# A longer pitch for the x, r and g tiles of an attention and feed-forward kernel, and two buffers of combined weight words

## The chip, the core and the metric

The kernel runs on one core of a Trainium2 chip. A core has five engines that run beside each other and wait for one another by semaphores: TensorE (PE; its weight loads are listed apart as PEld), VectorE (DVE), ScalarE (ACT), GpSimd (POOL) and SyncE (SP), whose queue starts nearly all transfers here. The on-chip memory has 128 partitions; an address in this document is a byte offset within each partition. The metric is device time in microseconds; less is better.

## What is computed

Linear attention over 8 batches, 8 heads, 576 positions and head size 64, and then a feed-forward network on its output (4608 tokens, 512 wide, 2048 hidden):

```python
q_s = exp(q - max(q, -1));  q_s = q_s / (sum(q_s, -1) + 1e-9)
k_s = exp(k - max(k, 2));   k_s = k_s / (sum(k_s, 2) + 1e-9)
kv = einsum('bhsd,bhse->bhde', k_s, v)
attn = einsum('bhsd,bhde->bhse', q_s, kv)
x = attn.transpose(0, 2, 1, 3).reshape(4608, 512)
h = x @ w_in
r = maximum(h, 0)
g = r * r
out = g @ w_out
```

All is float32, in and out.

## The kernel before

**Precision.** TensorE multiplies in the fast form of float32 (`F32R`). To keep accuracy, every operand of the feed-forward part is split in two: `hi`, the value cast to F32R, and `lo`, what is left. A product is made of three matmuls: hi × hi, hi × lo and lo × hi.

**Tiling.** Tokens go in 9 blocks: block 0 to 7 hold 512 of each batch's 576 positions, and block 8 the 64 left over of each batch, which attention parks in DRAM (`x_left`). x of a block lies in `x_hi` and `x_lo`, tiles of 128 partitions × 4 chunks (`cc`) × 512 tokens. There are two of each, and block `blk` uses number `blk % 2`: `x_hi0`, `x_lo0` in even blocks, `x_hi1`, `x_lo1` in odd ones. The second pair is made late (L527, L528), in the space that the tiles of the start (`first`) leave. A chunk of x is 512 × 4 = 2048 bytes, and each chunk follows the last at once.

The hidden width goes in 16 chunks (`fc`). One step is one block and one chunk, so there are 9 × 16 = 144 steps. A step is

- `ffn_h` (L412 to L414): for each of 4 chunks `cc`, three matmuls with 128 × 128 weights from `wi[fc]` as the loaded operand and x as the moving one, 512 columns: hi × x_hi, hi × x_lo, lo × x_hi. Twelve in all, called the x part below.
- `activate`: ScalarE takes the bank to `r` (L418, relu); VectorE squares it in place (L424; L422 in block 0); ScalarE casts it to `g_hi` (L425); VectorE, in most steps of block 0 GpSimd, subtracts to get `g_lo` (L429).
- `ffn_out` (L446 to L448), two steps later (`LAG`): for each of 4 groups of tokens, three matmuls with 128 columns of `g_hi`, `g_hi`, `g_lo` as the loaded operand and the 512 columns of `wo[fc]` hi, lo, hi as the moving one. Twelve in all, called the output part.

So a step has 24 matmuls of 512 columns, and each has a weight load of its own. All wi and wo stay on the chip: 4096 bytes each, 2048 of hi and 2048 of lo.

**Weights at the start.** During the start and block 0 each of the 32 weight chunks is made from raw bits by `split_weight`: ScalarE and VectorE combine the words in a buffer `w` (VectorE, L173, writes it last), then ScalarE casts it to the hi part (L180) and GpSimd subtracts to get the lo part (L181). `w` rotates over `WB` = 3 buffers of 2048 bytes.

**Attention** of the next block is cut into units that a table of numbers (`STEADY_AT`, `EARLY_AT`) puts between the steps. Its last matmuls (L384) have 320 or 256 columns, with `kvs` loaded and `qs` moving, and its results are split into the next block's x tiles. Block 7 only makes block 8's x from the parked tokens (`left_units`, L192 and L195), and block 8 has no attention beside it.

The order on each engine comes from a scheduler at build time. Tiles are laid out in the order of their pools, one after the other.

Of the kernel before, what the change touches and what calls it, by code (L numbers as in the profile page):

```python
# [8 lines left out]
F32 = mybir.dt.float32  # L9
F32R = mybir.dt.float32r  # L10
# [6 lines left out]
P = 128  # L17
# [2 lines left out]
HIGH = 4  # L20
BLK = 32
PAD = 8

half = slice(0, HALF), slice(HALF, P)
FLT_MAX = float.fromhex("0x1.fffffep127")
RAWB, WB = 4, 3

BESIDE = 4
EARLY_SPLITS = [("o",0),("o",1)]
# [16 lines left out]
def attention_ffn_kernel(ctx: ExitStack, tc: tile.TileContext, q, k, v, w_in, w_out, out):  # L46
# [5 lines left out]
    NCC = DM // P  # L52
    NFC = DF // P
    NT = 512
# [3 lines left out]
    const = ctx.enter_context(tc.tile_pool(name="const", bufs=1))  # L58
    work = ctx.enter_context(tc.tile_pool(name="work", bufs=2))
# [5 lines left out]

    stay = ctx.enter_context(tc.tile_pool(name="stay", bufs=1))
    raws, wi, wo = {}, {}, {}
    x_hi = [const.tile([P, NCC, NT], F32R, name="x_hi0")]
    x_lo = [const.tile([P, NCC, NT], F32R, name="x_lo0")]
    x_left = dram.tile([P, NCC, B * LEFT], F32, name="x_left")  # L70


# [25 lines left out]
    ones = const.tile([P, 1], F32, name="ones")  # L98
    const.tile([P, PAD], F32, name="pad_back")

# [313 lines left out]
        last.append(nc.tensor.matmul(ps, wi[fc][:, 1, sl], xh[:, cc, :], start=False, stop=(cc == NCC - 1)))  # L414

    def activate(ps, blk, fc):
        r = work.tile([P, NT], F32, name="r")
        nc.scalar.activation(r, ps, AF.Relu)  # L418
        g_hi = work.tile([P, NT], F32R, name="g_hi")
        g_lo = work.tile([P, NT], F32R, name="g_lo")  # L420
        if blk == 0:
            nc.vector.tensor_tensor(r, r, ps, op=ALU.mult)  # L422
        else:
            nc.vector.tensor_tensor(r, r, r, op=ALU.mult)  # L424
        gh = nc.scalar.copy(g_hi, r)  # L425
        if blk == 0:
            his.append(gh)
        e = nc.gpsimd if blk == 0 and fc < G_LOW_POOL else nc.vector
        e.tensor_tensor(g_lo, r, g_hi.bitcast(F32), op=ALU.subtract)  # L429
        return g_hi, g_lo  # L430

    def ffn_h(blk, fc):
        ps = next_bank("h" if blk else "first")
        for cc in range(NCC):
            h_part(ps, blk, fc, cc)
        return activate(ps, blk, fc)
# [87 lines left out]
    start_done.append(1)  # L524
    ps_o = ctx.enter_context(tc.tile_pool(name="ps_o", bufs=4, space=bass.MemoryType.PSUM))
    late = ctx.enter_context(tc.tile_pool(name="late", bufs=1))
    x_hi.append(late.tile([P, NCC, NT], F32R, name="x_hi1"))  # L527
    x_lo.append(late.tile([P, NCC, NT], F32R, name="x_lo1"))  # L528

    for pr in range(NB):  # L530
        load_pair(1, pr)
# [34 lines left out]
    for n in range(len(steps) + LAG):  # L566
        if n < len(steps):
            blk, fc = steps[n]
            if n < PRE:
                gs[n] = activate(hs[fc], blk, fc)  # L570
            else:
                gs[n] = ordered(ffn_h, blk, fc) if blk == 0 else ffn_h(blk, fc)
            if blk == 0:
                for x in [n + 4] if n else range(5):
                    if PRE <= x < NFC and order0[x] not in wi:
                        split_weight("i", order0[x])
                for x in [n + 2] if n else range(3):
                    if x < NFC and order0[x] not in wo:
                        split_weight("o", order0[x])
                finish_split()  # L580
        m = n - LAG
        in_slot(2 * n)
        if m >= 0:
            b2, f2 = steps[m]
            if m % NFC == 0:
                accs[b2] = [ps_o.tile([P, DM], F32, name=f"o_ps{t}", tag="o") for t in range(4)]
            args = b2, f2, gs.pop(m), accs[b2], m % NFC
            ordered(ffn_out, *args) if b2 == 0 else ffn_out(*args)
        in_slot(2 * n + 1)
# [30 lines left out]
```

## Time and profile before

| | us |
|---|---|
| median of 2 runs | 899.95 (899.69 to 900.2) |
| profiled execution | 900.7 |
| span of the profiled execution, first to last instruction | 898.9 |
| TensorE busy in it | 869.5 |
| mean granted TensorE clock | 0.994 |

The profile is of one execution. Its views used here are: the page (busy time by engine, 40 slices of the span, the chain of work that ended last), the windows (busy time by engine in a stretch), the groups by line and shape (busy us and mean ns of one, then the idle time of the engine ahead of them and what ended it), and the timeline (start in us, duration in us, engine, line, operation, tiles). A line number is that of the kernel before. A matmul's duration in the timeline overlaps the next one's, as TensorE is a pipeline and the ends are modelled; how fast matmuls go is read from the distance of their starts.

### The profile page before, as it was taken

The page shows a single profiled execution, that of the slowest core. Times are in us where ns is not written, and L with a number is a line of the kernel's source. Part 1 is how long each engine was busy: PE and PEld are TensorE (multiplying, and loading weights), DVE is VectorE, ACT ScalarE, POOL GpSimd, SP SyncE. Part 2 cuts the span into 40 slices and gives each one's busy share as a digit, 9 for nine tenths or more (in the row PEclk, how much of TensorE's full clock was granted, in tenths as well). Part 3 has the DMA queues.
Part 4 walks back from the last instruction along what each step waited for, and adds up shares of the span by engine and source line. Part 5 has one row for each costly group of instructions (what it writes and reads, how often), then busy time and mean ns, then how long its engine had stood idle before and what let it go on. Part 6 is the DMA issues. An engine that isn't in the chain of part 4 may idle for free.

```text
span 898.9 us, 12680 instructions
## 1 busy us (share of the span) xinstructions
PE 869.5 (97%) x4368; PEld 700.6 (78%) x4368; DVE 579.6 (64%) x1177; ACT 407.7 (45%) x801; POOL 202.4 (23%) x177
## 2 busy tenths in 40 slices
PE   4997999999999999999999999999999999999997
PEld 3675677888888888888888888888888888888885
DVE  7767898877778876877688767876764242222222
ACT  3785756455345453544454544454444232222222
POOL 3676634222212220231122212221222000000000
PEclk9998999999999999999999999999999999999999
DMA  9999212422142224322333133222311030002001
GB/s 234 278 317 257 68 30 58 117 77 79 44 117 76 80 58 104 85 71 71 88 84 81 51 83 88 77 66 69 92 31 32 2 93 1 1 1 47 1 1 47
DMA packets 95743, 73.18 MB, mean 81 GB/s; under 512 B 47552, under 2 KB 85440, under 8 KB 95680
## 3 DMA queue, kind: packets, MB, share of 16 engines
q1 hardware_dynamic: 94944, 71.53, 29.5%
q10 hardware_dynamic: 736, 0.85, 0.4%
q8 instruction: 34, 0.56, 0.3%
q14 instruction: 29, 0.24, 0.1%
HBM read 54.00 MB, written 18.35 MB: 80 GB/s over the span
## 4 chain that ended last, share of the span: by engine, by line
PE 85%; DVE 1%; issue 0%; ACT 0%
PE o_ps L446 14%; PE bank L412 14%; PE o_ps L448 14%; PE o_ps L447 14%; PE bank L414 13%; PE bank L413 13%; PE bank L305 2%; PE bank L384 1%; DVE w L173 0%; DVE r L422 0%; DVE bank L172 0%; DVE m L243 0%; DVE kvn L321 0%; DVE o_last L460 0%; DVE m L246 0%
## 5 line engine op out<-in xcount | busy, mean ns | idle before, releaser
L412 PE MATMUL bank<-x_hi,wi 128*128 128x512 f32 x568 | 226.0, 398 | 2.2 <-DVE r L422 2.2
L446 PE MATMUL o_ps<-wo,g_hi 128*128 128x512 f32 x576 | 227.6, 397 | 0.0
L447 PE MATMUL o_ps<-wo,g_hi 128*128 128x512 f32 x576 | 224.9, 390 | 0.0
L448 PE MATMUL o_ps<-wo,g_lo 128*128 128x512 f32 x576 | 224.4, 391 | 0.0
L414 PE MATMUL bank<-x_hi,wi 128*128 128x512 f32 x568 | 223.4, 393 | 0.0
L413 PE MATMUL bank<-x_lo,wi 128*128 128x512 f32 x568 | 222.4, 392 | 0.0
L424 DVE TENSOR_TENSOR r<-r 128x512 f32<-128x512 f32 x128 | 110.7, 865 | 119.5 <-ACT r L418 119.2
L429 DVE TENSOR_TENSOR g_lo<-r,g_hi 128x512 fp32r<-128x512 f32 x132 | 100.7, 763 | 106.7 <-ACT g_hi L425 105.3
L425 ACT CAST g_hi<-r 128x512 fp32r<-128x512 f32 x144 | 89.2, 619 | 124.4 <-PE o_ps L447 78.2
L418 ACT ACTIVATE r<-bank 128x512 f32<-128x512 f32 x142 | 84.7, 596 | 102.5 <-PE bank L414 99.6
L412 PEld LDWEIGHTS bank<-x_hi,wi 128*128 128x128 f32 x568 | 107.1, 189 | 26.3 <-DVE r L422 3.5
L446 PEld LDWEIGHTS o_ps<-wo,g_hi 128*128 128x128 f32 x576 | 108.2, 188 | 23.5 <-issue 0.5
L448 PEld LDWEIGHTS o_ps<-wo,g_lo 128*128 128x128 f32 x576 | 108.1, 188 | 23.2
L447 PEld LDWEIGHTS o_ps<-wo,g_hi 128*128 128x128 f32 x576 | 108.2, 188 | 22.8 <-issue 0.5
L414 PEld LDWEIGHTS bank<-x_hi,wi 128*128 128x128 f32 x568 | 106.9, 188 | 24.2 <-POOL wi L181 0.4
L413 PEld LDWEIGHTS bank<-x_lo,wi 128*128 128x128 f32 x568 | 107.0, 188 | 21.9 <-issue 0.2
L395 POOL TENSOR_TENSOR x_lo<-xf,x_hi 128x256 fp32r<-128x256 f32 x48 | 39.6, 825 | 374.0 <-ACT x_hi L394 373.3
L338 POOL TENSOR_TENSOR qs<-qT,qs 64x640 fp32r<-64x640 f32 x48 | 81.8, 1705 | 60.0 <-ACT qs L337 47.1
L224 DVE TENSOR_REDUCE m<-kt 128x128 f32<-128x640 f32 x32 | 41.4, 1298 | 20.6 <-DMA kt<-in_k_dram 20.4
L337 ACT CAST qs<-qT 64x640 fp32r<-64x640 f32 x48 | 34.9, 726 | 39.6 <-DMA qT<-bounce 39.0
L271 ACT ACTIVATE qn<-qn 128x640 f32<-128x640 f32 x32 | 23.6, 739 | 54.2 <-DVE qn L268 44.8
L386 ACT COPY xf<-bank 64x320 f32<-64x320 f32 (+1 forms) x96 | 37.9, 395 | 20.6 <-PE bank L384 13.0
(118 smaller groups left out, 775.3 us busy)
## 6 DMA issues: line engine op xcount, KB each, us to landing
out_dram<-o SPq DMA_DIRECT2D x70, 128.0 KB, 2.4
raw_i<-in_moe_w_in_dram SPq DMA_DIRECT2D x16, 512.0 KB, 8.4
raw_o<-in_moe_w_out_dram SPq DMA_DIRECT2D x16, 512.0 KB, 9.6
bounce<-tb SPq DMA_DIRECT2D x24, 320.0 KB, 2.2
qT<-bounce SPq DMA_DIRECT2D x96, 80.0 KB, 2.2
kt<-in_k_dram SPq DMA_DIRECT2D x32, 160.0 KB, 3.0
qt<-in_q_dram SPq DMA_DIRECT2D x30, 160.0 KB, 3.0
vt<-in_v_dram SPq DMA_DIRECT2D x56, 80.0 KB, 2.5
```

Source lines behind the costliest of these rows:

```text
L224: nc.vector.tensor_reduce(m, kk.rearrange("p h j d -> p h d j"), axis=AX.X, op=ALU.max)
L338: nc.gpsimd.tensor_tensor(qs[other], qT[own], qs[own].bitcast(F32), op=ALU.subtract)
L412: nc.tensor.matmul(ps, wi[fc][:, 0, sl], xh[:, cc, :], start=(cc == 0), stop=False)
L413: nc.tensor.matmul(ps, wi[fc][:, 0, sl], xl[:, cc, :], start=False, stop=False)
L414: last.append(nc.tensor.matmul(ps, wi[fc][:, 1, sl], xh[:, cc, :], start=False, stop=(cc == NCC - 1)))
L418: nc.scalar.activation(r, ps, AF.Relu)
L424: nc.vector.tensor_tensor(r, r, r, op=ALU.mult)
L425: gh = nc.scalar.copy(g_hi, r)
L429: e.tensor_tensor(g_lo, r, g_hi.bitcast(F32), op=ALU.subtract)
L446: nc.tensor.matmul(acc[t], g_hi[:, ts], wo[fc][:, 0], start=(n == 0), stop=False)
L447: nc.tensor.matmul(acc[t], g_hi[:, ts], wo[fc][:, 1], start=False, stop=False)
L448: prev = nc.tensor.matmul(acc[t], g_lo[:, ts], wo[fc][:, 0], start=False, stop=(n == NFC - 1))
```

## The change

Each chunk of the x tiles, and each of the tiles r, g_hi and g_lo, gets 64 bytes more behind its 2048 (`GAP` = 16 elements); the kernel takes the first 512 columns of it as before. A tile of 32 bytes (`pad_late`) is put ahead of `x_hi1`. The combined words `w` have two buffers and not three, which gives 2048 bytes back.

```diff
+GAP = 16
-RAWB, WB = 4, 3
+RAWB, WB = 4, 2
-    x_hi = [const.tile([P, NCC, NT], F32R, name="x_hi0")]
-    x_lo = [const.tile([P, NCC, NT], F32R, name="x_lo0")]
+    x_hi = [const.tile([P, NCC, NT + GAP], F32R, name="x_hi0")[:, :, :NT]]
+    x_lo = [const.tile([P, NCC, NT + GAP], F32R, name="x_lo0")[:, :, :NT]]
...
-        r = work.tile([P, NT], F32, name="r")
+        r = work.tile([P, NT + GAP], F32, name="r")[:, :NT]
...
-        g_hi = work.tile([P, NT], F32R, name="g_hi")
-        g_lo = work.tile([P, NT], F32R, name="g_lo")
+        g_hi = work.tile([P, NT + GAP], F32R, name="g_hi")[:, :NT]
+        g_lo = work.tile([P, NT + GAP], F32R, name="g_lo")[:, :NT]
...
-    x_hi.append(late.tile([P, NCC, NT], F32R, name="x_hi1"))
-    x_lo.append(late.tile([P, NCC, NT], F32R, name="x_lo1"))
+    late.tile([P, PAD], F32, name="pad_late")
+    x_hi.append(late.tile([P, NCC, NT + GAP], F32R, name="x_hi1")[:, :, :NT])
+    x_lo.append(late.tile([P, NCC, NT + GAP], F32R, name="x_lo1")[:, :, :NT])
```

Where the tiles begin in the built programs (bytes in each partition, and the same modulo 2048; r, g and w have several buffers):

| tile | before | modulo 2048 | after | modulo 2048 |
|---|---|---|---|---|
| x_hi0 | 1152 | 1152 | 1152 | 1152 |
| x_lo0 | 9344 | 1152 | 9600 | 1408 |
| r | 38208, 40256 | 1344, 1344 | 38720, 40832 | 1856, 1920 |
| g_hi | 42304, 44352 | 1344, 1344 | 42944, 45056 | 1984, 0 |
| g_lo | 46400, 48448 | 1344, 1344 | 47168, 49280 | 64, 128 |
| w | 63808, 65856, 67904 | 320 | 64704, 66752 | 1216 |
| wi, wo (first of 32, 4096 apart) | 80192 | 320 | 79040 | 1216 |
| x_hi1 | 211264 | 320 | 210144 | 1248 |
| x_lo1 | 219456 | 320 | 218592 | 1504 |

Chunk cc of an x tile lies 2048·cc behind its start before, and 2112·cc after: modulo 2048, all four at one place before, each 64 bytes further after.

On every engine the instructions stand in the same order in both programs; what differs is addresses, and what some wait for. The waits that are other ones are in block 0: two subtractions to g_lo on GpSimd name an earlier instruction of GpSimd itself, and the rest are in the combining of weights. Here is VectorE's queue before, around the writing of w for the first wo (SCALAR_TENSOR_TENSOR w<-raw_o is the last step of combining the words; in brackets stand the semaphores that a row waits for):

```order
L314 RECIPROCAL rs<-rs 128x1 [waits DVE_49]
L172 SCALAR_TENSOR_TENSOR bank_89<-bank_89,raw_o_165 128x512 [waits DMAHW4_49,Activation_49]
L173 SCALAR_TENSOR_TENSOR w<-raw_o_165,bank_89 128x512 [waits DVE_49]
L224 TENSOR_REDUCE m<-kt_78 128x128 [waits DMAHW5_49,DMAHW4_49]
L172 SCALAR_TENSOR_TENSOR bank_89<-bank_89,raw_o_169 128x512 [waits DMAHW6_49,Activation_49]
```

The same place after, where the lines stand one further down:

```order
L315 RECIPROCAL rs<-rs 128x1 [waits DVE_49]
L173 SCALAR_TENSOR_TENSOR bank_89<-bank_89,raw_o_165 128x512 [waits DMAHW4_49,Activation_49]
L174 SCALAR_TENSOR_TENSOR w<-raw_o_165,bank_89 128x512 [waits DVE_49,Pool_49]
L225 TENSOR_REDUCE m<-kt_78 128x128 [waits DMAHW5_49,DMAHW4_49]
L173 SCALAR_TENSOR_TENSOR bank_89<-bank_89,raw_o_169 128x512 [waits DMAHW6_49,Activation_49]
```

Nothing moved; the writing of w waits for GpSimd (Pool) too. The same is added at three more rows of this kind; at the other 28 the row waits for GpSimd already, or for nothing of it in either program, and where it waits, it is for the buffer two splits back and not three.

## The prediction

> **What bounds the kernel now.** I read the page first: busy shares, slices, the chain that ended last.
>
> ```profile
> PE 869.5 (97%) x4368; PEld 700.6 (78%) x4368; DVE 579.6 (64%) x1177; ACT 407.7 (45%) x801; POOL 202.4 (23%) x177
> ...
> PE   4997999999999999999999999999999999999997
> ...
> PEclk9998999999999999999999999999999999999999
> ...
> PE 85%; DVE 1%; issue 0%; ACT 0%
> ```
>
> TensorE is the bound from about the seventh slice on, at full granted clock, and 85% of the chain is its own work. A nanosecond more on every 512-column matmul therefore arrives at the end in full. The windows by stage say the same, and show where it is not so:
>
> ```profile
> 100.00:150.00 50.00, 47.12 (x233) 35.65 (x232) 44.64 (x91) 34.15 (x65) 26.38 (x19) 1.00 0.19 52
> 150.00:200.00 50.00, 50.00 (x256) 40.64 (x255) 39.36 (x83) 23.86 (x48) 12.07 (x9) 1.00 0.34 88
> ```
>
> (Columns: PE, PEld, DVE, ACT, POOL busy, clock, DMA share, GB/s.) Until 150 us TensorE still idles; behind it, it has no gap. So only blocks 1 to 8 (128 steps, 3072 matmuls of 512 columns) count for a price per matmul.
>
> Since no instruction moves, I then looked for anything that already depends on addresses. Block number mod 2 picks x_hi0/x_lo0 or x_hi1/x_lo1, and nothing else in the feed-forward part changes with it. The timeline of ScalarE has one L425 row per step (144 in all); these are the first of blocks 2 to 6 and 7:
>
> ```profile
> 247.35 0.62 ACT L425 CAST g_hi<-r 128x512 fp32r<-128x512 f32 x1 [1.89 <-PE o_ps L447]
> ...
> 341.62 0.62 ACT L425 CAST g_hi<-r 128x512 fp32r<-128x512 f32 x1 [1.84 <-PE o_ps L447]
> ...
> 435.30 0.62 ACT L425 CAST g_hi<-r 128x512 fp32r<-128x512 f32 x1 [1.89 <-PE o_ps L447]
> ...
> 529.56 0.62 ACT L425 CAST g_hi<-r 128x512 fp32r<-128x512 f32 x1 [1.84 <-PE o_ps L447]
> ...
> 623.11 0.62 ACT L425 CAST g_hi<-r 128x512 fp32r<-128x512 f32 x1 [1.89 <-PE o_ps L447]
> ...
> 717.39 0.62 ACT L425 CAST g_hi<-r 128x512 fp32r<-128x512 f32 x1 [1.84 <-PE o_ps L447]
> ```
>
> The differences are 94.27, 93.68, 94.26, 93.55, 94.28 us: even blocks take 0.655 us more (94.27 against 93.615), 41 ns a step. Without attention beside it the gap is cleaner. Block 7 from its 7th to its 13th step, and block 8 from its first to its last:
>
> ```profile
> 750.03 0.62 ACT L425 CAST g_hi<-r 128x512 fp32r<-128x512 f32 x1 [1.84 <-PE o_ps L447]
> ...
> 782.67 0.62 ACT L425 CAST g_hi<-r 128x512 fp32r<-128x512 f32 x1 [1.84 <-PE o_ps L447]
> ...
> 804.52 0.62 ACT L425 CAST g_hi<-r 128x512 fp32r<-128x512 f32 x1 [1.89 <-PE o_ps L447]
> ...
> 887.51 0.62 ACT L425 CAST g_hi<-r 128x512 fp32r<-128x512 f32 x1 [1.89 <-PE o_ps L447]
> ```
>
> Six steps in 32.64 us are 5.440 us each, 226.7 ns a matmul; 15 steps in 82.99 are 5.533, 230.5 ns. The same shapes at the same clock differ by 93 ns a step, and of the operands only x lies elsewhere. I call 226.7 the settled rate. How it is lost is seen one matmul at a time (timeline of TensorE, first column the start), in block 3 around an attention matmul:
>
> ```profile
> 348.98 0.39 PE L413 MATMUL bank<-x_lo,wi 128*128 128x512 f32 x1
> 349.20 0.39 PE L414 MATMUL bank<-x_hi,wi 128*128 128x512 f32 x1
> 349.43 0.31 PE L384 MATMUL bank<-qs,kvs 128*128 128x320 f32 x1
> 349.57 0.40 PE L412 MATMUL bank<-x_hi,wi 128*128 128x512 f32 x1
> ...
> 350.51 0.39 PE L413 MATMUL bank<-x_lo,wi 128*128 128x512 f32 x1
> 350.73 0.39 PE L414 MATMUL bank<-x_hi,wi 128*128 128x512 f32 x1
> 350.96 0.31 PE L384 MATMUL bank<-qs,kvs 128*128 128x320 f32 x1
> ```
>
> One foreign operand pair, and the six matmuls from 349.57 to 350.96 take 231.7 ns each. And where block 8 passes from the output part to x:
>
> ```profile
> 843.27 0.40 PE L412 MATMUL bank<-x_hi,wi 128*128 128x512 f32 x1
> 843.50 0.40 PE L413 MATMUL bank<-x_lo,wi 128*128 128x512 f32 x1
> 843.74 0.39 PE L414 MATMUL bank<-x_hi,wi 128*128 128x512 f32 x1
> ```
>
> Two intervals of together 0.47 us, 235 ns each: the dearest seen in a run of full matmuls.
>
> My reading: while a matmul streams its moving operand, the next one's weights are loaded, and how these two addresses stand to each other sets the rate. Modulo 512 bytes that distance is 0 in the output part (g loaded at 1344, wo streamed at 320) and in x parts on x_hi1 (320 and 320); in x parts on x_hi0 (1152) it is 192. With distance 0 throughout it settles; each change of distance unsettles it for some matmuls, and at 192 it does not settle.
>
> **The change part by part.**
>
> *Pitch and places of x.* As built, wi and wo start at 1216 modulo 2048. Chunk cc of x_hi0 then streams at 1152+64cc, x_lo0 at 1408+64cc, x_hi1 at 1248+64cc, x_lo1 at 1504+64cc. The distance, constant within a part before, now changes with every chunk, between hi and lo, and in odd blocks is 32 modulo 64, which no row of before shows. *Places of g.* g_hi lies at 1984 or 0, g_lo at 64 or 128: the distance to wo is now 256 or 320 for hi, 384 or 448 for lo, never 0. So no part keeps the only relation that I see settled. The price goes by two ends. Lower: odd blocks become as even ones are. Blocks 1, 3, 5: 3 × 0.655 = 1.97 us; block 7: 3 steps beside attention at 0.041 and 13 without at 0.093, 1.33 us. Sum 3.3 us. Upper: every matmul at the unsettled 231.7. Even blocks run at 230.5 (block 8's rate, taken for all), odd ones beside attention at 230.5 − 41/24 = 228.8. Blocks 2, 4, 6, 8: 1.2 × 384 × 4 = 1.84 us; blocks 1, 3, 5: 2.9 × 384 × 3 = 3.34; block 7: 72 × 2.9 + 312 × 5.0 = 1.77 us. Sum 6.9 us. I stay near the lower end, +4.1 us, since that is measured over whole blocks and the upper over six matmuls.
>
> A gain isn't excluded, as the 32-byte and 256-byte distances may settle too; that is a rival below.
>
> *Vector and scalar engines.* r, g, x and w move for them too. Here are their rows by shape in block 7:
>
> ```profile
> L424 DVE TENSOR_TENSOR r<-r 128x512 f32<-128x512 f32 x14 | 9.7, 691 | 28.4 <-ACT r L418 28.4
> L429 DVE TENSOR_TENSOR g_lo<-r,g_hi 128x512 fp32r<-128x512 f32 x14 | 9.7, 691 | 21.8 <-ACT g_hi L425 21.7
> ...
> L195 DVE TENSOR_TENSOR x_lo<-xs,x_hi 128x512 fp32r<-128x512 f32 x4 | 2.7, 690 | 2.0 <-ACT x_hi L192 2.0
> ```
>
> 691, 691 and 690 ns, though the inputs lie in three arrangements: one address twice, two tiles of equal phase, and xs against x at four different phases. I cost it at nothing; and VectorE's 28.4 us of idle time before L424 would cover a few per cent.
>
> *Two buffers of w.* L173 now waits until GpSimd's subtraction (L181) of two splits ago has read its buffer, not three. Behind the wait stands VectorE's queue in block 0, and behind that the r and k operations that TensorE waits for before 150 us. The least room that I find among 30 such pairs is this one:
>
> ```profile
> 60.32 1.30 POOL L181 TENSOR_TENSOR wi<-w,wi 128x512 fp32r<-128x512 f32 x1 [1.11 <-ACT wi L180]
> ...
> 63.34 0.69 DVE L173 SCALAR_TENSOR_TENSOR w<-raw_i,bank 128x512 uint32<-128x512 uint32 x1
> ```
>
> The read ends at 61.62, the write starts at 63.34: 1.72 us to spare. Cost 0; if that cover were gone, a 1.3 us subtraction late 30 times would be the bound, 39 us in block 0, from which these rows are far.
>
> Sum: the profiled execution took 900.7 us (span 898.9 and 1.8 around it); + 4.1 is 904.8. It stood 0.75 over the median of 899.95, so against the median 904.0.
>
> **The rivals.**
>
> *It settles better (faster).* If the new distances settle as 0 does, even blocks lose their extra: 3 × 0.655 + 16 × 0.093 = 3.5 us, 896.5. If attention matmuls no longer unsettle them either, another (228.8 − 226.7) × 384 × 6 = 4.8 us: 891.7. For it: only two distances have been seen, and one of two settles. Against: settling took a constant distance, and there is none now.
>
> *Addresses don't matter (no change).* Then 900.0. For it: the DVE rows above. Against: 5.440 and 5.533 us. [...] The trace does not agree where only x's place differs, 226.7 against 230.5 ns, so I give it less than it would have alone.
>
> *It never settles and each matmul is as dear as a first one (slower).* At 235 ns: even blocks 4.5 × 384 × 4 = 6.9 us, blocks 1, 3, 5 6.2 × 384 × 3 = 7.1, block 7 72 × 6.2 + 312 × 8.3 = 3.0; 17 us, 917. It decides against the change by over 2% only from a mean of about 235.4 ns on, with a further cost of the 32-byte shift in odd blocks.
>
> *The floor itself falls (much faster).* If 226.7 ns holds a conflict too, and the shortest interval above, 350.51 to 350.73 (0.22 us), were kept, 3072 × about 9.5 ns (from a mean of some 229.5 over blocks 1 to 8) would go: 871. Against: that short one follows a long one, and no mean of several lies below 226.7. [...]
>
> **How the numbers follow.** Unsettled more often, 901.5 to 909: 0.45. Settled better, 889 to 898.5: 0.27. No effect, within 1.5 us: 0.18. The floor falls: 0.05. Slower by over 2%: 0.05. The range 890 to 910 leaves out both last ones and the edges; the forecast's own is 901.5 to 909. About 2% is what a measurement of this kernel can tell from no change, so: faster 0.05, within 0.90, slower 0.05.
>
> **What would show it.** Right: L425 steps in block 7's end at about 5.53 us or more, where they were 5.440; blocks 3 and 5 as long as 2, 4, 6; intervals in groups of 226 to 235 ns in the output part too. L173 without a wait for GpSimd; DVE rows at 691. Wrong: steps of 5.44 in block 8 (settled better), both unchanged (no effect), any step under 5.4 (the floor), DVE or ACT rows that change, or a longer time to the first step of block 1.

## The result, and the profile after

| | before | after |
|---|---|---|
| median, us | 899.95 (2 runs) | 910.08 (2 runs, 909.85 to 910.3) |
| profiled execution, us (span) | 900.7 (898.9) | 909.85 (908.1) |
| ratio to before | | 1.0102, 95% interval 1.0082 to 1.0122 |

The changed kernel is slower by 1.0%. The forecast was 904.0, with a range of 890 to 910 and a range of its own of 901.5 to 909: the sign was right, and the size was more than double what was forecast, just outside both ranges.

The page of the kernel after has the same shape as before. TensorE's busy time has grown by 10.8 us, from 869.5; that of the other engines moved by no more than 1.2:

```profile
PE 880.3 (97%) x4368; PEld 702.7 (77%) x4368; DVE 580.8 (64%) x1177; ACT 407.8 (45%) x801; POOL 201.4 (22%) x177
...
PEclk9998999999999999999999999999999999999999
```

The clock row is that of before, and the mean granted clock is 0.995 where it was 0.994, so it is not the clock. ScalarE's timeline, the casts to g_hi (now L426, one line down) with which blocks 2 to 7 begin, one of the middle of block 7, and the first and last of block 8:

```profile
248.67 0.62 ACT L426 CAST g_hi<-r 128x512 fp32r<-128x512 f32 x1 [1.89 <-PE o_ps L448]
...
343.66 0.62 ACT L426 CAST g_hi<-r 128x512 fp32r<-128x512 f32 x1 [1.88 <-PE o_ps L448]
...
438.63 0.62 ACT L426 CAST g_hi<-r 128x512 fp32r<-128x512 f32 x1 [1.89 <-PE o_ps L448]
...
533.62 0.62 ACT L426 CAST g_hi<-r 128x512 fp32r<-128x512 f32 x1 [1.88 <-PE o_ps L448]
...
628.59 0.62 ACT L426 CAST g_hi<-r 128x512 fp32r<-128x512 f32 x1 [1.89 <-PE o_ps L448]
...
723.63 0.62 ACT L426 CAST g_hi<-r 128x512 fp32r<-128x512 f32 x1 [1.88 <-PE o_ps L448]
...
762.60 0.62 ACT L426 CAST g_hi<-r 128x512 fp32r<-128x512 f32 x1 [1.89 <-PE o_ps L448]
...
796.00 0.62 ACT L426 CAST g_hi<-r 128x512 fp32r<-128x512 f32 x1 [1.89 <-PE o_ps L448]
...
812.69 0.62 ACT L426 CAST g_hi<-r 128x512 fp32r<-128x512 f32 x1 [1.89 <-PE o_ps L448]
...
896.44 0.62 ACT L426 CAST g_hi<-r 128x512 fp32r<-128x512 f32 x1 [1.90 <-PE o_ps L448]
```

Blocks 2 to 6 take 94.99, 94.97, 94.99, 94.97 and 95.04 us: the difference between even and odd is gone, and all are longer than the longest of before (94.28). In block 7, six steps take 796.00 − 762.60 = 33.40 us, 5.567 each, where they were 5.440; in block 8, 15 steps take 83.75, 5.583 each, where they were 5.533. Against before, blocks 2, 4 and 6 have lost 0.72, 0.73 and 0.76 us, blocks 3 and 5 1.29 and 1.42, block 7 (812.69 − 723.63 = 89.06 against 87.13) 1.93, block 8 0.76 in 15 steps. With 1.44 in block 1 (from 154.18 to 248.67; before, from 154.30 to 247.35) that is 9.05 of the 9.2 us between the spans. Block 0 ends where it ended.

TensorE's timeline in block 7 after, first column the start, at the end of an x part and in the output part behind it:

```profile
764.48 0.39 PE L415 MATMUL bank<-x_hi,wi 128*128 128x512 f32 x1
764.71 0.40 PE L413 MATMUL bank<-x_hi,wi 128*128 128x512 f32 x1
...
765.41 0.40 PE L447 MATMUL o_ps<-wo,g_hi 128*128 128x512 f32 x1
765.64 0.40 PE L448 MATMUL o_ps<-wo,g_hi 128*128 128x512 f32 x1
...
766.80 0.39 PE L447 MATMUL o_ps<-wo,g_hi 128*128 128x512 f32 x1
```

Ten intervals from 764.48 to 766.80 are 232 ns each on average, across both parts. Nothing settles any more.

### The profile page after: what moved, and what is told of

Same layout as the page of the kernel before. It is cut to its first block, busy times and chain, and to the rows that moved or that the text cites. A ratio compares the mean times of both kernels' runs of the same rounds, so it can differ in the third digit from the quotient of the medians.

```text
span 908.1 us, 12684 instructions
## 1 busy us (share of the span) xinstructions
PE 880.3 (97%) x4368; PEld 702.7 (77%) x4368; DVE 580.8 (64%) x1177; ACT 407.8 (45%) x801; POOL 201.4 (22%) x177
## 4 chain that ended last, share of the span: by engine, by line
PE 87%; DMA 4%; DVE 4%; issue 1%; SPq 1%; ACT 1%; POOL 0%; DVEq 0%; POOLq 0%; ACTq 0%
PE bank L413 14%; PE o_ps L447 14%; PE bank L414 14%; PE o_ps L449 14%; PE bank L415 14%; PE o_ps L448 14%; PE bank L306 2%; DMA kt<-in_k_dram 2%; PE bank L385 1%; DMA qt<-in_q_dram 1%; DMA raw_i<-in_moe_w_in_dram 1%; DVE m L225 1%; SPq L154 1%; DVE bank L173 1%; PE first_ps L306 0%
## 5 line engine op out<-in xcount | busy, mean ns | idle before, releaser
L413 PE MATMUL bank<-x_hi,wi 128*128 128x512 f32 x568 | 227.5, 401 | 2.0 <-DVE r L423 1.9
L449 PE MATMUL o_ps<-wo,g_lo 128*128 128x512 f32 x576 | 226.9, 396 | 0.0
L414 PE MATMUL bank<-x_lo,wi 128*128 128x512 f32 x568 | 225.6, 397 | 0.0
L425 DVE TENSOR_TENSOR r<-r 128x512 f32<-128x512 f32 x128 | 112.7, 880 | 125.1 <-ACT r L419 124.7
L426 ACT CAST g_hi<-r 128x512 fp32r<-128x512 f32 x144 | 89.1, 619 | 123.2 <-PE o_ps L448 79.5
L387 ACT COPY xf<-bank 64x320 f32<-64x320 f32 (+1 forms) x96 | 38.0, 395 | 23.4 <-PE bank L385 17.4
```

Source lines behind the costliest of these rows:

```text
L413: nc.tensor.matmul(ps, wi[fc][:, 0, sl], xh[:, cc, :], start=(cc == 0), stop=False)
L414: nc.tensor.matmul(ps, wi[fc][:, 0, sl], xl[:, cc, :], start=False, stop=False)
L449: prev = nc.tensor.matmul(acc[t], g_lo[:, ts], wo[fc][:, 0], start=False, stop=(n == NFC - 1))
```

## The experiments

All have two buffers of w where nothing else is said, and all keep the order of instructions on every engine. "Distance" is the address of the weights being loaded minus that of the operand then streaming. Ratios are to runs of the kernel before on the same chip, where its median was 900.5 to 901.4 us. A step's time is read, as above, from ScalarE's casts to g_hi. The first four runs take the change apart.

**Two buffers alone.**

```diff
-RAWB, WB = 4, 3
+RAWB, WB = 4, 2
```

> The kernel before with two buffers of combined words and nothing else; all tiles behind them move by 2048 bytes, so every address modulo 2048 stays. Theory (the distance between the moving operand and the weights loaded beside it, modulo 512, sets the rate): no change, 900.0 within 0.5 us, steps of 5.440 us in block 7 and 5.533 in block 8. Rival (the loss comes from the missing third buffer): some 910, with VectorE waiting for GpSimd in block 0 and a later first step of block 1 than 154.3 us.

Measured: 901.07 us, ratio 1.0005 (0.9995 to 1.0014), steps of 5.44 and 5.53. The buffers cost nothing that can be told. In the changed kernel too VectorE does not wait for them: the profile names no wait ahead of any of its 32 rows that write w (L174). Here are GpSimd's timeline and VectorE's there, at the tightest pair of the prediction:

```profile
60.57 1.30 POOL L182 TENSOR_TENSOR wi<-w,wi 128x512 fp32r<-128x512 f32 x1 [1.10 <-ACT wi L181]
```

```profile
63.64 0.69 DVE L174 SCALAR_TENSOR_TENSOR w<-raw_i,bank 128x512 uint32<-128x512 uint32 x1
```

The read ends at 61.87, 1.77 us ahead of the write.

**All distances at 0, pitch as before.**

```diff
-    const.tile([P, PAD], F32, name="pad_back")
+    const.tile([P, PAD + 80], F32, name="pad_back")
```

> Two buffers of combined words, and 320 bytes more in the pad behind the constants, so that r, g, w, wi, wo and the odd x tiles all move by 320 and every distance, that of x_hi0 to wi too, is 0 modulo 512; pitch 2048 as before. Theory: block 8 settles, 5.44 us a step as in block 7; even blocks as long as odd ones (93.6 us); sum 896.5 within 1 us. Rival (x_hi0 is slow for its own address or for what is near it, not for the distance): 900, block 8 at 5.53.

Measured: 896.38 us, ratio 0.9959 (0.9944 to 0.9974). Here are ScalarE's first and last cast of block 8:

```profile
801.59 0.62 ACT L425 CAST g_hi<-r 128x512 fp32r<-128x512 f32 x1 [1.83 <-PE o_ps L447]
...
883.19 0.62 ACT L425 CAST g_hi<-r 128x512 fp32r<-128x512 f32 x1 [1.83 <-PE o_ps L447]
```

15 steps in 81.60 us: 5.440 each, where x_hi0 at its old distance had 5.533. x_hi0 itself did not move; the weights loaded beside it did. Nor is it the weights' own address, since odd blocks run at 5.440 with the weights at either place. So it is the distance. This kernel beats both.

**The pitch of x alone.**

```diff
-    x_hi = [const.tile([P, NCC, NT], F32R, name="x_hi0")]
+    x_hi = [const.tile([P, NCC, NT + GAP], F32R, name="x_hi0")[:, :, :NT]]
...
-    x_hi.append(late.tile([P, NCC, NT], F32R, name="x_hi1"))
+    x_hi.append(late.tile([P, NCC, NT + GAP], F32R, name="x_hi1")[:, :, :NT])
```

(x_lo likewise.)

> Two buffers of combined words, and the pitch of 2112 bytes for the x tiles alone, without the 32 bytes ahead of x_hi1; r and g as before, and their distance to wo still 0 modulo 512. Theory: the x part is unsettled in all blocks and the output part begins unsettled each time, as in block 8 of the kernel before or worse: steps of 5.53 to 5.58 us in blocks 7 and 8, 903 to 908 us. Rival (the places of g make the loss): 900 or less, block 7 at 5.44.

Measured: 905.73 us, ratio 1.0057 (1.0040 to 1.0074), 5.53 us a step in blocks 7 and 8. One x part in block 7 shows more, since its four chunks stand at four distances (TensorE's timeline):

```profile
760.80 0.39 PE L413 MATMUL bank<-x_hi,wi 128*128 128x512 f32 x1
761.03 0.39 PE L414 MATMUL bank<-x_lo,wi 128*128 128x512 f32 x1
761.25 0.39 PE L415 MATMUL bank<-x_hi,wi 128*128 128x512 f32 x1
761.48 0.40 PE L413 MATMUL bank<-x_hi,wi 128*128 128x512 f32 x1
...
762.89 0.40 PE L413 MATMUL bank<-x_hi,wi 128*128 128x512 f32 x1
```

The first chunk (hi at distance 0, lo at 256 modulo 512) keeps 0.68 us for three matmuls, 227 ns each; the six behind it (at 192 and then at 128 modulo 256) take 1.41, 235 ns each. So 256 is as good as 0, which suggested a period of 256 bytes and not 512. From here on, distances are given modulo 256.

**The pitch of r and g alone.**

```diff
-        r = work.tile([P, NT], F32, name="r")
+        r = work.tile([P, NT + GAP], F32, name="r")[:, :NT]
...
-        g_hi = work.tile([P, NT], F32R, name="g_hi")
-        g_lo = work.tile([P, NT], F32R, name="g_lo")
+        g_hi = work.tile([P, NT + GAP], F32R, name="g_hi")[:, :NT]
+        g_lo = work.tile([P, NT + GAP], F32R, name="g_lo")[:, :NT]
```

> Two buffers of combined words, and the pitch of 2112 bytes for r and g alone; x as before, so x_hi1 stands at distance 0 to wi, x_hi0 at 64 modulo 512, and g at 256 to 448 to wo. Theory: the output part is unsettled in all blocks, the x part of odd blocks can settle again: 5.47 to 5.55 us a step in block 7, 902 to 907 us. Rival (the pitch of x or the 32 bytes make the whole loss): 900, block 7 at 5.44.

Measured: 907.87 us, a little over what was expected, ratio 1.0084 (1.0069 to 1.0099), 5.507 us in block 7 and 5.58 in block 8. In this kernel x_hi0 stands at 64 where it stood at 192, so even blocks carry that too. Each of the two pitches makes a good part of the loss; together they make less than their sum (0.57 and 0.84% against 1.02%). In block 7 the pitch of x adds 93 ns to a step, that of g 67, and the change 127, which is 33 less than both. Of these 33, 19 are the output part in the run with the pitch of x (at distance 0, but 228.3 ns a matmul behind its unsettled x part), and 10 the x part in this run (at distance 0, 227.5 ns). In the changed kernel both parts stand off already, so this is not paid twice.

The next four ask which distances are good, and what else may count.

**A scan of distances.** Each weight chunk is 32 bytes longer, so the next one's distance is another:

```diff
-        raw = stay.tile([P, 512, 2], U32, name=f"raw_{part}{fc}", tag=f"{part}{fc}")
+        raw = stay.tile([P, 1024 + STEP], U32, name=f"raw_{part}{fc}", tag=f"{part}{fc}")[:, :1024].rearrange("p (f w) -> p f w", w=2)
...
-        chunk = stay.tile([P, 2, 512], F32R, name=f"w{part}{fc}", tag=f"{part}{fc}")
+        chunk = stay.tile([P, 1024 + STEP], F32R, name=f"w{part}{fc}", tag=f"{part}{fc}")[:, :1024].rearrange("p (t f) -> p t f", t=2)
```

> Two buffers of combined words, and 32 bytes more behind each weight chunk, so that the distances go through all multiples of 32 from step to step, constant within each x part and each output part. Theory, with the period that the run with the pitch of x alone suggests (its first chunk, at distances 0 and 256, kept 226.7 ns): the last matmuls of a part keep 226.7 ns where the distance is a multiple of 256 and nowhere else; the other distances lie at 228 to 235, the odd multiples of 32 too. Rival (a period of 64 or 128 bytes, or 32 as good as 0): 226.7 at other distances as well. A rate under 226.7 at some distance would say that the settled rate is no floor.

Measured, in a single run: 910.85 us beside 901.4. From TensorE's timeline in block 8, where no other work is beside it, a part's time is its first start to the first start of the next part, over 12 (steps 4 to 15):

| distance | part | ns a matmul |
|---|---|---|
| 0 | output | 231.5, the eleventh interval at 227 |
| 32 | x | 232.7 |
| 64 | output | 233.5 |
| 96 | x | 234.1 |
| 128 | output | 232.1 |
| 160 | x | 232.5 |
| 192 | output | 229.6 |
| 224 | x | 232.8 |

The part at 64 (g against wo) reads so:

```profile
872.65 0.39 PE L448 MATMUL o_ps<-wo,g_hi 128*128 128x512 f32 x1
...
874.98 0.40 PE L449 MATMUL o_ps<-wo,g_lo 128*128 128x512 f32 x1
```

Ten intervals in 2.33 us, 233 ns each from the second to the twelfth matmul: a constant distance, and no sign of settling. 192, the one that x_hi0 had before, is the cheapest of the seven distances other than 0, and all the rest cost 232 to 234. In this run the part at 0 is no cheaper: it stands behind an x part at 96 and needs ten matmuls to come down. That 0 is the good distance is seen where it is kept throughout, at 226.7 in the aligned kernel. No part lies under that.

**The 32 bytes ahead of x_hi1.** The changed kernel without them:

```diff
-    late.tile([P, PAD], F32, name="pad_late")
```

> The changed kernel without the 32 bytes ahead of x_hi1, so that in odd blocks the distances are multiples of 64 again. Theory: they still change from chunk to chunk and g is still off, so little comes back: 907 to 910 us, 5.54 to 5.58 us a step in block 7. Rival (the 32 bytes are what made the result dearer than forecast): 904 or less, block 7 under 5.50.

Measured: 909.96 us, ratio 1.0100 (1.0085 to 1.0115); 5.560 us a step in block 7 on average, where the changed kernel has 5.567. The 32 bytes add nothing that can be told in the total, and the scan agrees: 32 is about as bad as 64.

**A pitch of 2304 bytes with all distances at multiples of 256.**

```diff
-PAD = 8
+PAD = 8
+GAP = 64
...
-    const.tile([P, PAD], F32, name="pad_back")
+    const.tile([P, PAD + 16], F32, name="pad_back")
```

(GAP is added to r, g_hi, g_lo, x_hi1 and x_lo1 as in the change.)

> Two buffers of combined words, and a longer pitch that keeps all distances at multiples of 256: 2304 bytes for r, g and the odd x tiles, and 64 bytes more in the pad behind the constants, so that x_hi0 stands at 256 modulo 512 to wi. Theory with a period of 256: 896.4 as the aligned kernel, 5.44 us in blocks 7 and 8. Theory with a period of 512: blocks with x_hi0 stay slow, 5.53 in block 8, some 900. Rival (a pitch other than 2048 costs by itself): 903 or more.

Measured: 896.88 us, ratio 0.9953 (0.9936 to 0.9969), 5.44 us in blocks 7 and 8. A longer pitch costs nothing as such, and the period is 256: x_hi0 stands at 256 modulo 512 here and settles.

**Attention's matmuls too.** The aligned kernel, with kvs and qs moved by 128 bytes:

```diff
+    const.tile([P, 32], F32, name="pad_kvs")
     kvs = const.tile([P, 2, P], F32R, name="kvs")
...
-    const.tile([P, PAD], F32, name="pad_back")
+    const.tile([P, PAD + 48], F32, name="pad_back")
...
+    attn_pool.tile([P, 32], F32, name="pad_attn", bufs=1)
+    w_pool.tile([P, 32], F32, name="pad_w", bufs=1)
```

> The aligned kernel with kvs and qs of attention moved by 128 bytes as well, so that the 320-column attention matmuls and the loads of kvs stand at multiples of 256 to what runs beside them. Theory: a foreign matmul at distance 0 no longer unsettles the feed-forward ones; at most 4.8 us go, 892 to 895 us. Rival (any matmul of another length or of another kind unsettles, whatever its address): 896.4, as the aligned kernel.

Measured: 896.20 us, ratio 0.9946 (0.9929 to 0.9964): not to be told from the aligned kernel, and short of what was expected. TensorE's timeline behind an attention matmul (L387 here):

```profile
350.17 0.30 PE L387 MATMUL bank<-qs,kvs 128*128 128x320 f32 x1
350.32 0.40 PE L449 MATMUL o_ps<-wo,g_hi 128*128 128x512 f32 x1
...
351.69 0.39 PE L449 MATMUL o_ps<-wo,g_hi 128*128 128x512 f32 x1
```

The same place in the aligned kernel, where kvs and qs had not moved:

```profile
349.20 0.31 PE L384 MATMUL bank<-qs,kvs 128*128 128x320 f32 x1
349.34 0.39 PE L446 MATMUL o_ps<-wo,g_hi 128*128 128x512 f32 x1
...
350.72 0.39 PE L446 MATMUL o_ps<-wo,g_hi 128*128 128x512 f32 x1
```

Six matmuls take 1.37 us here and 1.38 there. Over the 68 places in blocks 1 to 6 where seven feed-forward matmuls or more stand behind one of these, the first six of their intervals average 229.7 ns here and 229.4 in the aligned kernel. So moving kvs and qs changed nothing that can be seen, and the rival of this run (any matmul of another length or kind unsettles, whatever its address) stands. The 4.8 us that I put on this were worked out from a mean over odd blocks and held other things. The float32 matmuls of attention (L305) unsettle too: in block 3 of the kernel before, behind 20 of them at 341.74, the ten intervals from 342.81 to 345.12 average 231 ns at distance 0, where settled ones take 226.7. Their tiles did not move here, and what moving them would give was not tried.

The last four check the reading itself.

**r alone at the longer pitch**, on the aligned kernel:

```diff
+GAP = 16
...
+    work.tile([P, 32], F32, name="pad_work", bufs=1)
...
-        r = work.tile([P, NT], F32, name="r")
+        r = work.tile([P, NT + GAP], F32, name="r")[:, :NT]
```

> The aligned kernel with the pitch of 2112 bytes for r alone (and 128 bytes of pad ahead of it, so that all that lies behind stays where it was modulo 256). TensorE never reads r. Theory: 896.4, 5.44 us a step in blocks 7 and 8, VectorE's squaring at 691 ns there. Rival (the places of r slow VectorE or ScalarE, and these TensorE): over 899.

Measured: 897.47 us, ratio 0.9962 (0.9947 to 0.9976), 5.44 us a step. VectorE's groups by shape in block 7:

```profile
L431 DVE TENSOR_TENSOR g_lo<-r,g_hi 128x512 fp32r<-128x512 f32 x14 | 9.7, 692 | 21.8 <-ACT g_hi L427 21.6
L426 DVE TENSOR_TENSOR r<-r 128x512 f32<-128x512 f32 x14 | 9.7, 692 | 28.6 <-ACT r L420 28.6
```

692 ns and 691 before. ScalarE's two rows on r stand at 600 and 622 ns, 597 and 624 before. So the places of r tried here matter neither to these engines nor to the total.

**Pitch 2048, every distance at 64.**

```diff
-    const.tile([P, PAD], F32, name="pad_back")
+    const.tile([P, PAD + 48], F32, name="pad_back")
...
+    w_pool.tile([P, 48], F32, name="pad_w", bufs=1)
...
+    late.tile([P, 48], F32, name="pad_late")
     x_hi.append(late.tile([P, NCC, NT], F32R, name="x_hi1"))
```

> Two buffers of combined words, pitch 2048 throughout as before, and pads of 192 bytes that put every distance, x to wi and g to wo, at 64 modulo 256, in all blocks and chunks alike. Theory as the scan corrects it (the distance itself sets the rate, 233.3 ns at 64): 5.60 us a step in blocks 7 and 8, 910 to 913 us, as slow as the changed kernel without any change of pitch. Rival, the wording of the prediction (a constant distance settles, changes of it unsettle): 5.44 us a step, 896.4.

Measured: 912.33 us, ratio 1.0129 (1.0114 to 1.0144), 5.593 us a step in blocks 7 and 8. ScalarE's first and last cast of block 8:

```profile
814.93 0.62 ACT L426 CAST g_hi<-r 128x512 fp32r<-128x512 f32 x1 [1.91 <-PE o_ps L448]
...
898.84 0.62 ACT L426 CAST g_hi<-r 128x512 fp32r<-128x512 f32 x1 [1.91 <-PE o_ps L448]
```

15 steps in 83.91 us. No pitch is changed and no distance changes within a part, and a step takes longer than in the changed kernel (5.567 and 5.583). So it takes no change of distance to keep matmuls unsettled. The prediction had said that of 192 alone, and argued from changes everywhere else.

**x_hi0 at 64 and not 192**, all else as before:

```diff
-    const.tile([P, PAD], F32, name="pad_back")
+    const.tile([P, PAD + 32], F32, name="pad_back")
```

> Two buffers of combined words, and 128 bytes more in the pad behind the constants, so that x_hi0 and x_lo0 stand at 64 modulo 256 to wi where they stood at 192; all else as before, odd blocks at 0. Theory as the scan corrects it (64 costs 233.3 ns, 192 only 229): block 8 at 5.56 to 5.59 us a step, block 7 at 5.44, even blocks 0.6 us longer, 902 to 904 us. Rival (all distances but 0 cost alike): 900, block 8 at 5.53.

Measured: 902.69 us, ratio 1.0018 (1.0008 to 1.0028); 5.54 us in block 8, 5.44 in block 7. The total is as expected, the step a little under it: the x part runs at 233.3 ns as at 64 in the scan, but the output part behind it settles sooner than behind 192 (228.3 ns on average). In the kernel before, an output part of block 8 runs from its first matmul to the next x part so:

```profile
846.03 0.40 PE L446 MATMUL o_ps<-wo,g_hi 128*128 128x512 f32 x1
...
848.80 0.40 PE L412 MATMUL bank<-x_hi,wi 128*128 128x512 f32 x1
```

That is 2.77 us, 230.8 ns a matmul at distance 0. So of the 93 ns by which an even step was longer, about half (49) was paid in the output part and not at 192 itself. The price of a distance is not read from its own part alone.

**How wide the good place is.** The aligned kernel, with wo chunks 8 to 15 moved by 8 to 248 bytes:

```diff
+ROOM = 64
+AT = {8: 2, 9: 4, 10: 8, 11: 12, 12: 24, 13: 56, 14: 60, 15: 62}
...
+        at = AT.get(fc, 0) if part == "o" else 0
+        chunk = stay.tile([P, 1024 + (ROOM if at else 0)], F32R, name=f"w{part}{fc}", tag=f"{part}{fc}")[:, at : at + 1024]
+        chunk = chunk.rearrange("p (t f) -> p t f", t=2)
```

> The aligned kernel with the wo chunks 8 to 15 moved by 8, 16, 32, 48, 96, 224, 240 and 248 bytes within longer tiles, so that only their output parts stand off, g to wo at minus these modulo 256. Theory: 226.7 ns in steps that use chunks 0 to 7, more in the others, down to shifts of 8 bytes or not that far: this run says how wide the good place is. Rival (226.7 is itself a partial conflict): some shift gives less than 226.7.

Measured, in a single run: 903.88 us beside 901.33. TensorE's timeline in block 8, the first matmul of the output part with chunk 7 (unmoved), that of the x part behind it, and the same with chunk 8 (8 bytes):

```profile
854.24 0.39 PE L452 MATMUL o_ps<-wo,g_hi 128*128 128x512 f32 x1
...
856.96 0.39 PE L418 MATMUL bank<-x_hi,wi 128*128 128x512 f32 x1
...
859.68 0.40 PE L452 MATMUL o_ps<-wo,g_hi 128*128 128x512 f32 x1
...
862.47 0.39 PE L418 MATMUL bank<-x_hi,wi 128*128 128x512 f32 x1
```

2.72 us against 2.79: 227 ns against 233 a matmul for 8 bytes. Moves of 16, 32, 48, 96, 224 and 240 bytes gave 231.4, 233.7, 233.4, 234.6, 233.6 and 233.3 in the same way, and 248, which is 8 bytes off on the other side, 232.4 in block 7. So the good place is narrow on both sides. No part lies under 226.7.

## Why the prediction was right in its way and wrong in its size

- *The place that bounds the time.* Right: TensorE's matmuls carry it, and the loss is spread over blocks 1 to 8 as a price per matmul (9.05 of 9.2 us), with none in block 0.
- *The address reading.* Right in kind: what counts is the distance of the loaded weights to the moving operand. The aligned kernel (896.38 us), the one at a pitch of 2304 (896.88) and the one at 64 throughout (912.33) show it, and neither r at another pitch (ratio 0.9962, where the aligned kernel has 0.9959) nor w at two buffers (1.0005) cost anything that can be told. Modulo 512 was too coarse: it is 256, as x_hi0 at 256 modulo 512 ran at 5.44 us a step, while 128 cost 232.1 ns in the scan. Modulo 256 the chunks of x in the changed kernel stand at 64, 0, 192 and 128 in even blocks and at 224, 160, 96 and 32 in odd ones, g_hi at 0 or 64, g_lo at 128 or 192. So "never 0" was wrong of one buffer of g_hi, and one chunk of x in even blocks stands at the good distance too. It helps that chunk little, as the next point shows.
- *"Each change of distance unsettles it."* Right as far as it goes. With the pitch of x alone, six matmuls behind changes to 192 and 128 took 235 ns each, where these distances cost 229.6 and 232.1 when kept. In the changed kernel's block 8, the chunk at distance 0 stands between two changes:

```profile
835.76 0.39 PE L413 MATMUL bank<-x_hi,wi 128*128 128x512 f32 x1
...
836.47 0.39 PE L413 MATMUL bank<-x_hi,wi 128*128 128x512 f32 x1
```

  Its three matmuls take 0.71 us, where three settled ones take 0.68. But most distances need no change to be dear (229.6 to 234.1 at the seven of the scan): a constant 64 stays at 233 ns to the end of the part there, and with all distances at 64 a step takes 5.593 us throughout blocks 7 and 8.
- *The sum, the step that failed.* The price of an unsettled matmul was too low, and at the lower end not every block paid one. That end, "odd blocks become as even ones are", put blocks 2, 4, 6 and 8 at nothing, and priced the others by the only other distance in the profile, 192, which the scan shows as the cheapest of seven (229.6 in the output part against 232 to 234). The upper end took 231.7 for every matmul, from six that were on their way back to settled; the changed kernel takes 231.9 at the end of block 7 and 232.6 in block 8. Measured, blocks 1, 3 and 5 lost 4.15 us (1.97 to 3.34 foreseen), blocks 2, 4, 6 and 8 2.97 (0 to 1.84), block 7 1.93 (1.33 to 1.77): 9.05 in the sum against 3.3 to 6.9. Going near the lower end "since that is measured over whole blocks" made it worse: many matmuls at one distance tell nothing of the other distances.
- *Vector and scalar engines.* Right: VectorE's rows in block 7 stand at 691 and 692 ns at the places tried, and ScalarE's within 3 ns.
- *Two buffers of w.* Right: no wait, 1.77 us to spare.
- *The rivals.* "Settles better" was false for this pitch, but what it foresaw of even blocks that settle came true in the aligned kernel: 3.5 us less were foreseen, and 4.1 measured (896.38 against 900.51, 95% interval 2.3 to 5.0). That the forecast 896.5 and the measured 896.38 lie closer still is luck, as the kernel before ran 0.6 us longer on that chip. "Addresses don't matter" fell: 8 bytes cost 6 ns a matmul (233 against 227). "The floor falls" found no support: of all distances tried, none went under 226.7. "As dear as a first one", 235 ns, was too dear by little: the changed kernel takes 232 to 233.

What stays open: why the rate depends on the distance with a period of 256 bytes. The runs show the rate by distance, and no cause in the memory or in TensorE. Nor do they tell whether a matmul's own weights count or the next one's, which are loaded while it streams (in block 7 of the kernel before, a load of 0.19 us begins at 763.88 with one matmul, and the matmul that uses it at 764.11): within most parts both lie at the same place modulo 256, and that it is the next one's is the reading of the prediction, not shown.

## What to carry to other kernels

Where TensorE is the bound and each matmul has its own weight load, compare the same step over blocks that use different buffers. Here steps of the same shapes differed by 93 ns, it was an address effect, and a pad of 320 bytes removed it (896.4 against 900.5 us). For such matmuls (F32R, 512 columns; for no others is it shown), choose pads so that the operand being streamed and the weights being loaded beside it begin at the same place modulo 256, for every chunk and buffer. A pitch 64 bytes longer, which broke this, lost (910.08 against 899.95 us), and one 256 bytes longer, which kept it, was free (896.88, where the aligned kernel has 896.38). A price seen at one bad place is not the price of another (229.6 ns at 192, 233.5 at 64): measure several before taking it for a bound.

## What the runs showed that I had not expected

- 8 bytes off the good place are as bad as 64 (233 against 227 ns).
- The cost is no smooth function of the distance: 229.6 ns at 192, 232.1 at 128, 233.5 at 64.
- The two halves of a step hang together: an output part at 0 took 228.3 ns a matmul behind an x part at 64, 230.8 behind one at 192 and 231.5 behind one at 96.
